# Two batches' first projections as one Strassen-Winograd product, in a fused attention and MLP kernel

## The chip, the cores and the metric

The kernel runs on one core of a Trainium2 chip. The metric is device time in microseconds (us); the kernel before takes 426.1 us (median of three runs, 425.94 to 427.35). The profiled execution, on which every reading below rests, spans 425.5 us at a mean TensorE clock of 0.992 of full speed. The engines are called as the profile calls them: PE is TensorE (PEld its weight loads), DVE is VectorE, ACT is ScalarE, POOL is GpSimd, SP is the engine that issues most transfers.

## What is computed

An attention with normalised queries and keys over 8 batches, 12 heads, 448 tokens and 64 elements a head, then an MLP on the 3584 tokens of width 768, with 2048 hidden columns and a gated activation.

```python
# q, k, v: (8, 12, 448, 64); w_in: (768, 2048); w_out: (2048, 768)
q_n, k_n = rmsnorm(q, g_q), rmsnorm(k, g_k)
attn = softmax(q_n @ k_n.T / 8) @ v                    # per batch and head
x = attn.transpose(0, 2, 1, 3).reshape(3584, 768)
h = x @ w_in                                           # the first projection
g = h * (1.0 / (1.0 + np.exp(-1.702 * h)))
out = g @ w_out                                        # the second projection
```

## The kernel before

Two heads make a pair, so there are 48 pairs, six per batch. Each pair is loaded, normalised, transposed and taken through scores, exponentials and values; six finished pairs make one batch's `xT` (768 x 448, as six blocks of 128 rows). Matrix products take bfloat16 operands and accumulate in float32.

Nothing is emitted in source order. Every piece of work is a task with an engine, an assumed duration, dependencies and a priority, and a small list scheduler written in the kernel's Python decides the order in which the instructions enter the program. The priorities (a table of 2,194 numbers named `KEYS`), the earliest starts of loads (`AT`) and a set of tasks that use another engine than the default one (`ON`) were found by a search. The hardware then runs each engine's instructions in that fixed order, each waiting for its own inputs.

```python
# the first projection of batch b, 128 hidden columns m, and what follows
def first(b, m, kis):
    if kis[0] == 0:
        gps[b, m] = bank()                          # one PSUM bank
    for j, (f, lo, n) in enumerate(blocks(b, m)):   # for b > 0: one block, n = 448
        for ki in kis:                              # 6 of them
            nc.tensor.matmul(gps[b, m][:, j * SH:j * SH + n],
                             lhsT=w_in_s[:, ki, f * 128:(f + 1) * 128],
                             rhs=xT[b][:, ki, lo:lo + n], start=(ki == 0), stop=(ki == KI - 1))

def tanh(b, m):
    th = ths[b, m] = th_p.tile([128, S], FP32, tag="th", name="th")
    nc.scalar.activation(out=th[:, :], in_=gps[b, m][:, :S], func=ACT.Tanh, scale=0.851)

def gate(b, m):                                     # g = (tanh + 1) * h; the 0.5 comes at the end
    ...
    nc.vector.scalar_tensor_tensor(
        out=g_of[b // 2][:, f:f + len(g), lo:lo + n], in0=view(ths.pop((b, m))[:, :]),
        scalar=1.0, in1=view(gps.pop((b, m))[:, :S]), op0=ALU.add, op1=ALU.mult)

# pairs from 12 on are transposed by a transfer; their q is multiplied by g on ScalarE
def scale_q(i):
    t = qk_ring[turn(i, N_KZ, K_KZ)][:, 0]
    nc.scalar.activation(out=t, in_=t, func=ACT.Identity, scale=gG[:, :])

# matmuls without use, put into gaps of TensorE early in the kernel, so that its clock stays up
FILL, FILL_GAPS = 0.9, 0.6
def fill(idle, now):
    ...
    n = idle * FILL / 213 if now < 14000.0 else idle * FILL_GAPS / 110
    for _ in range(int(n)):
        nc.tensor.matmul(banks[2][:, :256], lhsT=ident[:, :], rhs=zeros[:, :], start=True, stop=True)
```

The second projection is already a Strassen-Winograd product from batch 1 on. It takes two blocks of 128 tokens at a time (`pair`), with seven products of eight 128x384 matmuls where the plain way has eight. Its sums of `g` are made on VectorE (`add_up`), the combinations of `w_out` once (`combine`). Results that several outputs share stay in one PSUM bank, are copied out, and the next product is accumulated on top. The orders in which the parts enter are short lists; `FINAL` is that of the last two batches.

```python
EVEN = order("As A1 A2 A5 A6 C0 A7 C1 A4 A3")
MIDDLE = order("As A1 A2 A5 A6 C2 A7 C3 A4 A3 Bs B1 B2 B5 B6 D0 B7 D1 B4 B3")
FINAL = order("As A1 B1 A2 A5 A6 C2 A7 Bs C3 A4 A3 B2 B6 B5 B7 B8 B4")
```

Of the kernel before, what the change touches and what calls it, by code (L numbers as in the profile page):

```python
# [26 lines left out]
class _Order:  # L27
# [198 lines left out]
    'g': -8.99, 'gT': -17.52, 'gG': 7.12, ('S', 0, 0): 48.69, ('R', 0, 0): 7.11, ('S', 0, 1):  # L226
    60.39, ('R', 0, 1): 11.55, ('Q', 0): 58.96, ('N', 0, 0): 66.3, ('N', 0, 1): 7.12, ('V', 0):
    64.11, ('T', 0, 0): -21.71, ('T', 0, 1): -16.49, ('KQ', 0): 14.75, ('K', 0): 13.48, ('S', 1,
    0): 60.38, ('R', 1, 0): -9.0, ('S', 1, 1): 51.98, ('R', 1, 1): 17.35, ('Q', 1): 58.97, ('N',
    1, 0): 69.37, ('N', 1, 1): 66.3, ('V', 1): 7.13, ('T', 1, 0): 51.1, ('T', 1, 1): -27.7,  # L230
    ('KQ', 1): -1.35, ('K', 1): 4.81, ('S', 2, 0): 58.98, ('R', 2, 0): 13.51, ('Q', 2): 58.7,
    ('N', 2, 0): 70, ('N', 2, 1): -23.02, ('V', 2): 60.28, ('T', 2, 0): 28.84, ('T', 2, 1):
    -21.72, ('KQ', 2): 3.26, ('K', 2): -10.77, ('S', 3, 0): 67.81, ('R', 3, 0): 23.51, ('Q', 3):
    58.99, ('N', 3, 0): 66.13, ('N', 3, 1): 6.04, ('V', 3): -2.35, ('T', 3, 0): 51.09, ('T', 3,
    1): 40.36, ('KQ', 3): 5.81, ('K', 3): -15.4, ('S', 4, 0): 68.26, ('R', 4, 0): 7.79, ('Q',
    4): 47.82, ('N', 4, 0): 70, ('N', 4, 1): -17.48, ('V', 4): 58.38, ('T', 4, 0): -11.68, ('T',
    4, 1): 35.03, ('KQ', 4): 3.28, ('K', 4): 3.79, ('S', 5, 0): 68.27, ('R', 5, 0): -17.48,
    ('Q', 5): 47.88, ('N', 5, 0): 32.37, ('N', 5, 1): 4.32, ('V', 5): 56.71, ('T', 5, 0):
    -13.72, ('T', 5, 1): 46.07, ('KQ', 5): 3.27, ('K', 5): 10.41, ('L', 6, 0): -36.46, ('L', 6,
    1): -30.62, ('L', 6, 2): -30.26, ('S', 6, 0): 56.02, ('R', 6, 0): -10.86, ('N', 6, 0):  # L240
    63.85, ('N', 6, 1): -24.56, ('V', 6): -8.75, ('T', 6, 0): -26.04, ('T', 6, 1): -15.74,
    ('KQ', 6): 60.01, ('K', 6): 55.83, ('L', 7, 0): -33.93, ('L', 7, 1): -36.65, ('L', 7, 2):
    -30.27, ('S', 7, 0): 61.95, ('R', 7, 0): 53.79, ('N', 7, 0): 33.51, ('N', 7, 1): 37.76,
    ('V', 7): 1.98, ('T', 7, 0): 30.53, ('T', 7, 1): 19.28, ('KQ', 7): 70, ('K', 7): 69.99,
    ('L', 8, 0): -31.47, ('L', 8, 1): -30.61, ('L', 8, 2): -21.79, ('S', 8, 0): 66.7, ('R', 8,
    0): 15.23, ('Q0', 8): 11.01, ('Q', 8): -20.67, ('N', 8, 0): 33.53, ('N', 8, 1): -24.55,
    ('V', 8): 1.99, ('T', 8, 0): 25.89, ('T', 8, 1): -26.03, ('KQ', 8): 70, ('K', 8): 62.1,
    ('L', 9, 0): -22.78, ('L', 9, 1): -1.99, ('L', 9, 2): 21.48, ('S', 9, 0): -0.06, ('R', 9,
    0): 64.25, ('N', 9, 0): -14.38, ('N', 9, 1): -14.72, ('V', 9): 38.61, ('T', 9, 0): 6.15,
    ('T', 9, 1): -7.29, ('KQ', 9): 26.68, ('K', 9): 11.06, ('L', 10, 0): -2.06, ('L', 10, 1):  # L250
    -31.62, ('L', 10, 2): -30.35, ('S', 10, 0): 65.29, ('R', 10, 0): 56.16, ('N', 10, 0): -5.2,
    ('N', 10, 1): 8.16, ('V', 10): 60.31, ('T', 10, 0): -3.07, ('T', 10, 1): 15.45, ('KQ', 10):
    21.0, ('K', 10): 26.52, ('L', 11, 0): -1.91, ('L', 11, 1): 9.45, ('L', 11, 2): 3.39, ('S',
    11, 0): 38.83, ('R', 11, 0): 9.16, ('Q0', 11): 9.17, ('Q', 11): 14.55, ('N', 11, 0): -8.55,
    ('N', 11, 1): -8.56, ('V', 11): 32.03, ('T', 11, 0): -28.56, ('T', 11, 1): -11.34, ('KQ',
    11): 26.68, ('K', 11): -4.75, ('C', 0, 0, 0): 34.74, ('E', 0, 0, 0): 70, ('C', 0, 0, 1):
    37.36, ('E', 0, 0, 1): 58.69, ('P', 0, 0, 0, 0): -16.98, ('P', 0, 0, 0, 1): -33.13, ('P', 0,
    0, 0, 2): -27.68, ('P', 0, 0, 0, 3): 37.5, ('O', 0, 0, 0): -10.77, ('B', 0, 0): -11.23,
    ('X', 0, 0): -10.78, ('C', 1, 0, 0): -11.08, ('E', 1, 0, 0): 58.69, ('C', 1, 0, 1): 60.18,
    ('E', 1, 0, 1): 68.27, ('P', 1, 0, 0, 0): -21.73, ('P', 1, 0, 0, 1): 38.67, ('P', 1, 0, 0,  # L260
    2): -11.3, ('P', 1, 0, 0, 3): -29.83, ('O', 1, 0, 0): 3.27, ('B', 1, 0): 37.69, ('X', 1, 0):
    1.43, ('C', 2, 0, 0): 30.87, ('E', 2, 0, 0): 49.27, ('C', 2, 0, 1): 39.88, ('E', 2, 0, 1):
    69.95, ('P', 2, 0, 0, 0): -11.24, ('P', 2, 0, 0, 1): -11.3, ('P', 2, 0, 0, 2): 37.46, ('P',
    2, 0, 0, 3): 31.02, ('O', 2, 0, 0): 3.28, ('B', 2, 0): 17.36, ('X', 2, 0): -17.49, ('C', 3,
    0, 0): -18.24, ('E', 3, 0, 0): 67.04, ('C', 3, 0, 1): 50.92, ('E', 3, 0, 1): 47.91, ('P', 3,
    0, 0, 0): 31.97, ('P', 3, 0, 0, 1): -12.34, ('P', 3, 0, 0, 2): -13.73, ('P', 3, 0, 0, 3):
    32.17, ('O', 3, 0, 0): 3.05, ('B', 3, 0): -11.62, ('X', 3, 0): 6.39, ('C', 4, 0, 0): 33.09,
    ('E', 4, 0, 0): 66.44, ('C', 4, 0, 1): -27.1, ('E', 4, 0, 1): 66.38, ('P', 4, 0, 0, 0):
    32.0, ('P', 4, 0, 0, 1): -9.02, ('P', 4, 0, 0, 2): 29.97, ('P', 4, 0, 0, 3): 64.71, ('O', 4,
    0, 0): -10.87, ('B', 4, 0): 50.01, ('X', 4, 0): -0.66, ('C', 5, 0, 0): -25.89, ('E', 5, 0,  # L270
    0): 66.27, ('C', 5, 0, 1): -29.85, ('E', 5, 0, 1): 48.61, ('P', 5, 0, 0, 0): -10.94, ('P',
    5, 0, 0, 1): -29.62, ('P', 5, 0, 0, 2): -22.05, ('P', 5, 0, 0, 3): -16.54, ('O', 5, 0, 0):
    -7.38, ('B', 5, 0): -31.04, ('X', 5, 0): 2.32, ('C', 0, 1, 0): -20.61, ('E', 0, 1, 0):
    39.25, ('C', 0, 1, 1): 43.58, ('E', 0, 1, 1): 66.79, ('P', 0, 1, 0, 0): -11.67, ('P', 0, 1,
    0, 1): -13.09, ('P', 0, 1, 0, 2): 50.02, ('P', 0, 1, 0, 3): -27.45, ('O', 0, 1, 0): -11.7,
    ('B', 0, 1): 13.7, ('X', 0, 1): 7.23, ('C', 1, 1, 0): -36.95, ('E', 1, 1, 0): 45.11, ('C',
    1, 1, 1): 27.45, ('E', 1, 1, 1): 49.86, ('P', 1, 1, 0, 0): 15.35, ('P', 1, 1, 0, 1): -11.14,
    ('P', 1, 1, 0, 2): 49.86, ('P', 1, 1, 0, 3): -10.43, ('O', 1, 1, 0): 3.77, ('B', 1, 1):
    -14.37, ('X', 1, 1): 61.57, ('C', 2, 1, 0): -29.61, ('E', 2, 1, 0): 31.97, ('C', 2, 1, 1):
    -13.61, ('E', 2, 1, 1): 55.11, ('P', 2, 1, 0, 0): -4.79, ('P', 2, 1, 0, 1): -26.92, ('P', 2,  # L280
    1, 0, 2): -0.62, ('P', 2, 1, 0, 3): 14.23, ('O', 2, 1, 0): 2.31, ('B', 2, 1): 12.76, ('X',
    2, 1): 61.62, ('C', 3, 1, 0): -9.15, ('E', 3, 1, 0): 49.88, ('C', 3, 1, 1): 29.49, ('E', 3,
    1, 1): -5.68, ('P', 3, 1, 0, 0): -20.47, ('P', 3, 1, 0, 1): -26.35, ('P', 3, 1, 0, 2):
    -3.45, ('P', 3, 1, 0, 3): -26.51, ('O', 3, 1, 0): 56.03, ('B', 3, 1): -0.42, ('X', 3, 1):
    64.25, ('C', 4, 1, 0): 2.8, ('E', 4, 1, 0): 67.06, ('C', 4, 1, 1): -11.13, ('E', 4, 1, 1):
    40.1, ('P', 4, 1, 0, 0): 8.28, ('P', 4, 1, 0, 1): 4.99, ('P', 4, 1, 0, 2): 3.29, ('P', 4, 1,
    0, 3): -10.4, ('O', 4, 1, 0): 57.66, ('B', 4, 1): 25.6, ('X', 4, 1): 52.71, ('C', 5, 1, 0):
    -27.46, ('E', 5, 1, 0): 65.24, ('C', 5, 1, 1): -8.91, ('E', 5, 1, 1): 59.07, ('P', 5, 1, 0,
    0): 21.04, ('P', 5, 1, 0, 1): -24.61, ('P', 5, 1, 0, 2): 31.7, ('P', 5, 1, 0, 3): 19.29,
    ('O', 5, 1, 0): 52.63, ('B', 5, 1): -15.73, ('X', 5, 1): 56.53, ('C', 6, None, 0): 16.59,  # L290
    ('E', 6, None, 0): 52.49, ('E', 6, None, 1): -39.65, ('C', 6, None, 2): 4.04, ('E', 6, None,
    2): -4.25, ('E', 6, None, 3): -4.26, ('P', 6, None, 0, 0): -3.9, ('P', 6, None, 0, 1):
    -37.8, ('P', 6, None, 0, 2): -0.46, ('P', 6, None, 0, 3): -25.6, ('O', 6, None, 0): 52.95,
    ('P', 6, None, 1, 0): 1.59, ('P', 6, None, 1, 1): -0.0, ('P', 6, None, 1, 2): 7.1, ('P', 6,
    None, 1, 3): 14.16, ('O', 6, None, 1): 44.94, ('B', 6, None): -29.08, ('X', 6, None): 44.9,
    ('C', 7, None, 0): -15.8, ('E', 7, None, 0): -37.98, ('E', 7, None, 1): -37.64, ('C', 7,
    None, 2): -28.54, ('E', 7, None, 2): -36.42, ('E', 7, None, 3): -19.56, ('P', 7, None, 0,
    0): -2.06, ('P', 7, None, 0, 1): -27.45, ('P', 7, None, 0, 2): -27.46, ('P', 7, None, 0, 3):
# [543 lines left out]
def kernel(  # L842
# [635 lines left out]
    def copy_out(frm, bp, tm, hf):  # L1478
        nc.scalar.mul(half_of(bp, tm, hf), held[frm], 0.5)
# [249 lines left out]
```

## Time and profile before

| | busy us | share of the span |
|---|---|---|
| PE | 409.6 | 96% |
| PEld | 239.9 | 56% |
| DVE | 313.4 | 74% |
| ACT | 295.4 | 69% |
| POOL | 179.7 | 42% |

A row of the profile names the source line, the engine, what is written from what, the shape, the count, then busy time and the mean duration of one, then the engine's idle time before these instructions and what ended it. Busy time of PE counts pipelined matmuls to their modelled ends, so two matmuls that follow each other overlap in it. In a timeline the distance from one start to the next shows the pace; the printed length includes the depth of the pipeline. The rows and stages that the argument needs are shown with it below.

### The profile page before, as it was taken

To read this page: it belongs to the slowest core of one execution; us is meant where nothing else is said; L and a number is where in the kernel's file an instruction comes from. 1 tells how busy PE (TensorE), PEld (TensorE's weight loads), DVE (VectorE), ACT (ScalarE), POOL (GpSimd) and SP (SyncE) were. 2 spreads that over 40 slices of the span, in tenths; PEclk is the share of its full clock that TensorE was granted. 3 is DMA by queue.
4 is the path that set the end of the run, shared out by engine and by line. 5 is a ranking of instruction groups with operands and counts; after the bars stand their busy time and mean duration, and the time that the engine had idled before them with its cause. 6 is when DMAs were issued, how large, how long until landed. Compare 5 with 4: busy or idle time off the path is not lost.

```text
span 425.5 us, 9982 instructions
## 1 busy us (share of the span) xinstructions
PE 409.6 (96%) x3859; PEld 239.9 (56%) x3859; DVE 313.4 (74%) x608; ACT 295.4 (69%) x432; POOL 179.7 (42%) x258
## 2 busy tenths in 40 slices
PE   6989899999999999899999999999999999999995
PEld 4657787564455554565456655555555655555553
DVE  4878789569987979876898787875766655644663
ACT  4898587889979688858877788787966477304400
POOL 4677967674276887552553233242511000000000
PEclk9799999999999999999999999999999999999999
DMA  8999999869368787579657865467435450130023
GB/s 200 237 254 246 248 262 241 199 146 187 78 147 182 181 232 166 131 162 216 154 128 171 209 179 141 100 150 181 91 79 128 123 99 13 23 89 16 0 76 93
DMA packets 101556, 63.38 MB, mean 149 GB/s; under 512 B 54916, under 2 KB 101508, under 8 KB 101508
## 3 DMA queue, kind: packets, MB, share of 16 engines
q1 hardware_dynamic: 93712, 55.88, 55.3%
q0 software_dynamic: 7296, 6.29, 9.1%
q8 instruction: 30, 0.49, 0.5%
q10 hardware_dynamic: 500, 0.57, 0.4%
q14 instruction: 18, 0.15, 0.1%
HBM read 45.61 MB, written 11.01 MB: 133 GB/s over the span
## 4 chain that ended last, share of the span: by engine, by line
PE 76%; DVE 10%; DMA 9%; issue 2%; ACT 1%; POOL 1%; SPq 0%; DVEq 0%; ACTq 0%
PE w L1379 24%; PE w L1469 22%; PE o L1168 10%; PE sc L1147 8%; DMA w_in_s<-in_moe_w_in_dram 4%; PE sc L1379 4%; PE w L1409 3%; DVE g L1401 3%; PE sc L1469 2%; DMA late<-in_v_dram 2%; DVE late L1449 2%; DMA raw<-in_k_dram 1%; ACT th L1389 1%; DMA raw<-in_q_dram 1%; DVE ssq L1038 1%
## 5 line engine op out<-in xcount | busy, mean ns | idle before, releaser
L1155 ACT ACTIVATE att<-sc 112x896 bf16<-112x896 f32 x168 | 145.4, 915 | 33.0 <-PE sc L1147 32.4
L1379 PE MATMUL w<-xt,w_in_s 128*128 128x448 bf16 (+1 forms) x780 | 141.8, 329 | 2.5 <-DMA w_in_s<-in_moe_w_in_dram 1.4
L1379 PEld LDWEIGHTS <-w_in_s 128*128 128x128 bf16 x864 | 79.9, 98 | 62.1 <-issue 8.5
L1401 DVE SCALAR_TENSOR_TENSOR g<-th,w 128x448 bf16<-128x448 f32 x114 | 68.8, 616 | 26.5 <-ACT th L1389 26.1
L1080 POOL TENSOR_TENSOR row<-raw,rs 112x512 bf16<-112x512 f32 x65 | 72.3, 1130 | 31.2 <-DMA qk<-row 19.5
L1168 PEld LDWEIGHTS <-att 112*128 112x128 bf16 x1536 | 63.2, 98 | 31.3 <-issue 10.6
L1389 ACT ACTIVATE th<-w 128x448 f32<-128x448 f32 x114 | 61.4, 545 | 25.0 <-PE w L1379 22.6
L1038 DVE TENSOR_REDUCE ssq<-sq 112x16 f32<-112x1024 f32 (+1 forms) x50 | 58.2, 1170 | 11.5 <-ACT sq L1029 10.0
L1168 PE MATMUL o<-vx,att 112*128 112x65 bf16 x1280 | 60.7, 195 | 1.9 <-DVE obs L1179 1.9
L1093 POOL TENSOR_TENSOR vx<-vraw,ones 112x512 bf16<-112x512 f32 x22 | 23.8, 1082 | 89.7 <-PE o L1168 70.4
L1147 PE MATMUL sc<-qk 64*128 64x448 bf16 (+1 forms) x360 | 47.6, 344 | 0.1
L1469 PEld LDWEIGHTS <-g 128*128 128x128 bf16 x336 | 30.9, 98 | 22.2 <-issue 3.3
L1179 DVE TENSOR_TENSOR obs<-o,rcp 112x256 bf16<-112x256 f32 x96 | 40.8, 424 | 3.3
L1469 PEld LDWEIGHTS <-late 128*128 128x128 bf16 x328 | 29.9, 98 | 22.6 <-issue 4.0
L1029 ACT ACTIVATE sq<-raw 112x1024 f32<-112x1024 f32 (+1 forms) x32 | 31.8, 1002 | 5.8 <-DMA raw<-in_q_dram 4.3
L1469 PE MATMUL w<-w_out_s,g 128*128 128x384 bf16 x192 | 35.8, 326 | 0.0
L1178 DVE RECIPROCAL rcp<-o 112x4 f32<-112x4 f32 x96 | 17.0, 177 | 22.4 <-PE o L1168 22.0
L1026 POOL TENSOR_TENSOR sq<-raw 112x1024 f32<-112x1024 f32 x14 | 26.9, 1922 | 10.7 <-DMA raw<-in_k_dram 7.5
L1469 PE MATMUL w<-late 128*128 128x384 bf16 x152 | 28.5, 326 | 0.0
L1469 PE MATMUL w<-w_out_s,late 128*128 128x384 bf16 x144 | 27.5, 326 | 0.0
L1070 POOL TENSOR_TENSOR t<-rs 112x48 f32<-112x48 f32 x28 | 8.2, 292 | 42.5 <-DVE rs L1059 28.6
L1389 ACT ACTIVATE th<-sc 128x448 f32<-128x448 f32 x14 | 7.6, 543 | 26.5 <-PE sc L1379 21.7
(89 smaller groups left out, 436.8 us busy)
## 6 DMA issues: line engine op xcount, KB each, us to landing
raw<-in_q_dram SPq DMA_DIRECT2D x44, 224.0 KB, 3.8
raw<-in_k_dram SPq DMA_DIRECT2D x43, 224.0 KB, 4.3
vraw<-in_v_dram SPq DMA_DIRECT2D x42, 224.0 KB, 3.8
w_in_s<-in_moe_w_in_dram POOLq DMA_DIRECT2D x4, 768.0 KB, 15.0
w_out_s<-in_moe_w_out_dram POOLq DMA_DIRECT2D x4, 768.0 KB, 19.6
out_dram<-osb SPq DMA_DIRECT2D x13, 168.0 KB, 3.2
out_dram<-osb SPq DMA_DIRECT2D x12, 144.0 KB, 3.7
out_dram<-osb SPq DMA_DIRECT2D x12, 120.0 KB, 2.0
```

The lines of the kernel that those rows point to most:

```text
L1026: nc.gpsimd.tensor_tensor(out=sq[i % N_SQ][:SS, part], in0=raw[turn(i, N_RAW, K_RAW)][:SS, part], in1=raw[turn(i, N_RAW, K_RAW)][:SS, part ...
L1029: nc.scalar.activation(out=sq[i % N_SQ][:SS, part], in_=raw[turn(i, N_RAW, K_RAW)][:SS, part], func=ACT.Square)
L1038: nc.vector.reduce_sum(out=ssq_of[g0][:SS, i - g0, part], in_=sq[i % N_SQ][:SS, part], axis=AX.X)
L1080: eng.tensor_tensor(out=row_ring[i % N_QKN][:SS, gi].rearrange("p n (h d) -> p h n d", h=2), in0=raw[turn(i, N_RAW, K_RAW)][:SS, gi], in1= ...
L1147: nc.tensor.matmul(sc[:, hp, j * SH:j * SH + n], lhsT=qkw[r, k0:k0 + WIN], rhs=qk[r, 0, qs], start=True, stop=True)
L1155: nc.scalar.activation(out=att[:SS, t, :, :S], in_=sc, func=ACT.Exp)
L1168: nc.tensor.matmul(os_[u, w][:, x, :], lhsT=att_of(u)[:SS, kc, hp, qs * SS:qs * SS + WIN], rhs=vx_ring[turn(i, N_V, K_V)][:SS, hp, kc, :], ...
L1179: nc.vector.tensor_tensor(out=to[:SS, :, w, :] if h is None else to[:SS, :2].rearrange("p n h d -> p (n h) d"), in0=o[:SS, :, :D], in1=rcp ...
L1379: nc.tensor.matmul(gps[b, m][:, j * SH:j * SH + n], lhsT=w_in_s[:, ki, f * 128:(f + 1) * 128], rhs=xT[b][:, ki, lo:lo + n], start=(ki == 0 ...
L1389: nc.scalar.activation(out=th[:, :], in_=gps[b, m][:, :S], func=ACT.Tanh, scale=0.851)
L1401: nc.vector.scalar_tensor_tensor(out=g_of[b // 2][:, f:f + len(g), lo:lo + n], in0=view(ths.pop((b, m))[:, :]), scalar=1.0, in1=view(gps.p ...
L1469: nc.tensor.matmul(held[to], lhsT=lhs[:, ko, :], rhs=y[:, ko, :], start=first and ko == 0, stop=ko == NK - 1, skip_group_check=not first)
```

## The change

The first projections of batches 6 and 7 (called `B0` and `B1` in the code) become one product. Its two-by-two blocks are the two batches, the two halves of the 768 input columns and the two halves of the 2048 hidden columns. Strassen-Winograd forms it with seven block products in place of eight. A block product is, for 128 hidden columns `n` of eight, three matmuls of 128x448. Combinations of `w_in` (`w_term`) and of the two `xT` (`x_term`) are made on VectorE, in the space of the raw inputs once the attention no longer needs them.

```diff
+    W11, W21, W12, W22 = [w_in_s[:, KH * c:KH * c + KH, FH * r:FH * r + FH] ...]
+    W_TERMS = ((W3, W11, W21, ALU.subtract), (W21, W21, W22, ALU.add), (W2, W21, W11, ALU.subtract),
+               (W4, W12, W2, ALU.subtract))
+    def w_term(j, h):                  # j of 4, half h of 2: each 128 x 1536 bfloat16
+        ...
+        nc.vector.tensor_tensor(out=o, in0=x, in1=y, op=op)
+    def x_term(j):                     # 4 of them, each 128 x 1344 bfloat16
+        o, x, y = ((X1, x_half(B1, 0), x_half(B0, 0)),
+                   (x_half(B1, 0), x_half(B1, 1), x_half(B1, 0)),
+                   (X2, x_half(B1, 1), X1), (X4, x_half(B0, 1), X2))[j]
+        nc.vector.tensor_tensor(out=o, in0=x, in1=y, op=ALU.subtract)
+    def joint_product(n, j, to, first):
+        if first:
+            joint[n, to] = bank()
+        w, x = ((W11, x_half(B0, 0)), (W12, x_half(B0, 1)), (W4, x_half(B1, 1)), (W22, X4),
+                (W21, X1), (W2, X2), (W3, x_half(B1, 0)))[j - 1]
+        for ki in range(KH):           # KH = 3
+            nc.tensor.matmul(joint[n, to][:, :S], lhsT=w[:, ki, n * 128:(n + 1) * 128],
+                             rhs=x[:, ki, :], start=first and ki == 0, stop=ki == KH - 1, ...)
```

Products 1, 6, 7 and 4 share one bank. After 1, 6 and 7 the running sum is copied out (`part_copy`, by ScalarE or VectorE, as the scheduler picks); VectorE then adds another bank to the copy (`part_add`), and ScalarE makes the gelu in one instruction (`gelu`) from that sum, or from the bank itself after product 4. The two-step tanh and gate of these batches are gone, a second set of activation tables is loaded once, after the last exponential, and the last two batches' outputs no longer need the factor 0.5.

```diff
+    def gelu(b, f, src):
+        nc.scalar.activation(out=g_of[B // 2 - 1][:, f, (b - B0) * S:(b - B0 + 1) * S], in_=src(),
+                             func=ACT.Gelu_apprx_sigmoid)
-    FINAL = order("As A1 B1 A2 A5 A6 C2 A7 Bs C3 A4 A3 B2 B6 B5 B7 B8 B4")
+    for n in range(NF := MI // 2):     # 8 columns, staggered
+        FINAL += [(n, 1), (n, 2)] * (n > 0) + [(n - 2, 3)] * (n > 1) + [(n - 1, 7)] * (n > 0)
+        FINAL += [(n, 5), (n, 6)] + [(n - 1, 4)] * (n > 0)
+    FINAL += [(NF - 2, 3)] + order("Ax") + [(NF - 1, 7)] + order("Bx") + [(NF - 1, 4), (NF - 1, 3)]
+    FINAL += order("Ex Au Bu Ay Av By Bv As A5 A6 Ey A7 E2 A4 A3 Bs B5 B6 C0 B7 C1 B4 B3 Es C2 E6 C3 "
+                   "E5 E7 E8 E4")
```

The product of q with g moves to VectorE, and the fill ahead of 14 us grows.

```diff
-        nc.scalar.activation(out=t, in_=t, func=ACT.Identity, scale=gG[:, :])
+        nc.vector.tensor_scalar(out=t, in0=t, scalar1=gG[:, :], scalar2=None, op0=ALU.mult)
-    FILL, FILL_GAPS = 0.9, 0.6
+    FILL, FILL_GAPS = 1.2, 0.6
-    osb_ring = ring("osb", 6, [128, HALF], FP32)
+    osb_ring = ring("osb", 5, [128, S], FP32)
...
-    PACE = 5800.0
+    PACE, PACE_2, TURN = 5800.0, 4700.0, 71000.0
+    def now_key():
+        return 10.3 + min(done, TURN) / PACE + max(done - TURN, 0.0) / PACE_2
```

With these tasks the search over priorities, earliest starts and engines was run anew: all 2,194 old priorities have new values, and 49 are added. The `ON` set moves single normalisations, squares and casts between VectorE, GpSimd and ScalarE. Normalisations on VectorE go from 25 to 31, casts of v there from 20 to 18, squares on GpSimd from 15 to 12 (the rest run on ScalarE). Of the weight loads, which go through one queue one after the other, the earliest starts in the scheduler's table are these, in us:

| | w_in 0 | 1 | 2 | 3 | w_out 0 | 1 | 2 | 3 |
|---|---|---|---|---|---|---|---|---|
| before | 11.2 | 15.4 | 24.8 | 0 | 10.4 | 53.0 | 18.3 | 0 |
| after | 11.0 | 6.3 | 25.1 | 25.4 | 29.6 | 53.0 | 44.1 | 46.0 |

A later load in the chain can't start ahead of an earlier one, whatever its own entry.

## The prediction

> **What bounds the kernel now.** I read the page's busy shares first, then the TensorE timeline of the last stage, then who TensorE waited for, and last the windows early and late, to see what room the other engines have.
>
> On the page, TensorE is near full and everything else is not:
>
> ```profile
> PE 409.6 (96%) x3859; PEld 239.9 (56%) x3859; DVE 313.4 (74%) x608; ACT 295.4 (69%) x432; POOL 179.7 (42%) x258
> PE   6989899999999999899999999999999999999995
> PEclk9799999999999999999999999999999999999999
> ```
>
> A busy PE counts pipelined ends, so I checked it in the timeline of PE between 380 and 402 us (start, length, line, matmuls):
>
> ```profile
> 380.87 2.43 PE L1379 MATMUL sc<-xt,w_in_s 128*128 128x448 bf16 x12
> 383.13 2.43 PE L1379 MATMUL w<-xt,w_in_s 128*128 128x448 bf16 x12
> 385.40 1.30 PE L1379 MATMUL sc<-xt,w_in_s 128*128 128x448 bf16 x6
> 386.54 1.30 PE L1379 MATMUL w<-xt,w_in_s 128*128 128x448 bf16 x6
> 387.99 3.57 PE L1379 MATMUL sc<-xt,w_in_s 128*128 128x448 bf16 x18 [0.15 <-DVE g L1401]
> ...
> 399.65 2.76 PE L1469 MATMUL w<-w_out_s,g 128*128 128x384 bf16 x16
> 402.25 1.46 PE L1469 MATMUL sc<-w_out_s,g 128*128 128x384 bf16 x8
> ```
>
> Six matmuls of 448 columns take 386.54 - 385.40 = 1.14 us from start to start, 0.189 each; sixteen of 384 take 402.25 - 399.65 = 2.60, 0.1625 each. The groups touch. This stage runs at TensorE's pace, so a matmul less is its time less. From start distances over the whole timeline (start, plus length, less the 0.165 us by which touching groups overlap) I sum 14 us in which TensorE did nothing: 8.4 before 60 us, 3.8 between 100 and 180, 1.8 after 360. Its longest waits by name:
>
> ```profile
> PE o L1168 <- DVE obs L1179: 1.9, 4, 1.2
> PE w L1194 <- DVE obs L1179: 1.4, 2, 1.0
> ...
> PE w L1379 <- DMA w_in_s<-in_moe_w_in_dram: 1.4, 1, 1.4
> ...
> PE w L1379 <- DVE g L1401: 1.1, 3, 0.5
> ```
>
> Early on there is waste that isn't idle: the 74 fill matmuls on the page, 15.0 us busy and all before 35 us, while the first useful projection starts at 35.98 us. By their start distances they fill about 10 us. The last matmul ends near 421.2 us, and the last copy and store take the remaining 4.3.
>
> **What the Trainium skill says.** "TensorE: Matmul & The Clock Gate", section Part 1 on the clock gate, gives the warm start-to-start time as columns over 2.4 GHz plus about 2.5 ns. That is 189 and 162.5 ns for the two widths here; the trace agrees with both. "ScalarE: Activation LUTs", section "What ACT_TABLE_LOAD costs", says that every function costs the same per element, 186 ns plus 0.833 ns an element with immediate scale: 559 ns for 448, as an estimate for the new gelu. The trace has 545 for the tanh that it replaces, and two table loads of 1283 ns each. "VectorE: DVE Perf Modes" says in "Side-by-side" that a one-source bfloat16 operation in SBUF can take four elements a cycle with about 150 cycles of overhead: (112 + 158)/0.96 = 281 ns as an estimate for q times g. No run yet shows that form; the trace has ScalarE at 668 ns for it.
>
> **The change part by part.**
>
> *Matmuls.* Removed: 2 batches x 16 x 6 = 192 of 448 columns. Added: 8 x 7 x 3 = 168. The second projections keep their number, 3 pairs x 7 x 8 + 4 x 8 = 200 for the last two batches. So 24 x 0.189 = 4.54 us less on TensorE, all on the path.
>
> *New sums of inputs, on VectorE.* 8 `w_term` of 1536: the present combinations of w_out have this shape at 1147 ns (two of them 1692), so 8 x 1.15 = 9.2 us. 4 `x_term`, three of 1344: a 1024 sum takes 687 ns when not disturbed, hence 0.85 each, 3.4 in all. Only the last `x_term`s depend on the end of the attention.
>
> *Gates to gelus.* 32 gates x 0.616 = 19.7 us leave VectorE; 24 adds of the same shape come, 24 x 0.62 = 14.9. ScalarE changes 32 tanh for 32 gelus at the same cost, takes part of 24 copies (0.55 each) and one table load of 1.28.
>
> *q times g.* 36 x 0.668 = 24.0 us leave ScalarE; 36 x 0.28 = 10.1 come to VectorE.
>
> *Engines chosen anew.* Six more normalisations on VectorE (918 ns: +5.5), two casts less (680 ns: -1.4); three more squares on ScalarE (+3.0).
>
> *Where these land.* From the joint product on, TensorE has 168 x 0.189 + 200 x 0.1625 = 31.8 + 32.5 = 64.3 us of work without any attention in it. If the last matmul ends at 421.2 - 4.5 = 416.7, the joint product must start by about 352 us, whereas the attention's last values now run at 372.5. Two windows up to that point:
>
> ```profile
> 0.00:372.00 372.00, 361.34 (x3570) 212.91 (x3571) 285.75 (x559) 285.58 (x413) 179.65 (x258) 0.99 0.72 163
> 372.00:425.50 53.50, 48.30 (x291) 27.01 (x288) 27.66 (x50) 9.84 (x19) 0.00 (x0) 1.00 0.20 54
> ```
>
> VectorE (third pair) and ScalarE (fourth) both stand at 286 of 372, 77%. After: VectorE in all 313.4 + 9.2 + 3.4 - 19.7 + 14.9 + 10.1 + 5.5 - 1.4 = 335; less what follows the start of the joint product (24 adds 14.9, 13 sums x 0.69 = 9.0, some 18 output copies and adds x 0.557 = 10.0), 301 of 352, 86%. ScalarE: 295.4 - 24.0 + 3.0 + 6 (half the copies) = 280, less 32 x 0.55, the copies and a few outputs, 27: 253 of 352, 72%. So ScalarE gains room and VectorE loses it; it stays below its stage's length, but with less slack for TensorE's needs. In the joint stage itself one column block takes TensorE 21 x 0.189 = 3.97 us, against ScalarE's 4 x 0.55 + 1.5 x 0.55 = 3.0 and VectorE's 3 x 0.62 + 1.5 x 0.55 = 2.7. Both fit.
>
> *The chain in one bank.* A copy must end before the next product goes on top: about 0.1 + 0.55 + 0.1 us. The order leaves four other products (2.27 us) after products 1 and 6, but only two (1.14 us) between 7 and 4. That holds if the copy starts at once. A gelu ahead of it on ScalarE can cost some 0.3 us, at worst in each of eight blocks: 0 to 2.4 us; I take 0.8. At the end, product 3 of the last block needs add and gelu (0.62 + 0.56 + waits, 1.6 us); the second projections that don't need it last 1.95 us. Covered.
>
> *Start of the joint product.* `x_term` after the last transposed block, 3 us of transfer and 3 x 0.85 us on VectorE, is covered only if the order keeps enough second projections of batch 5 for it. The list places four products of 1.3 us there, with the new first two products among them. I put down 0.7 us lost.
>
> *New order.* It may win part of the 14 us idle and 10 us fill: the third and fourth w_in loads are allowed 3 us earlier than they were issued (28.4 and 29.3 us), and the 1.4 us wait for them should go. The stage between 100 and 180 us, where VectorE is at 84 to 97%, gets 0.28 us per pair more on VectorE and can lose. Net guess: 2.2 us won.
>
> The sum: 426.1 - 4.5 + 0.8 + 0.7 - 2.2 + 0.5 (more early fill and VectorE slack) = 420.6.
>
> **Rivals.**
>
> *VectorE becomes the bound in the middle.* For it: 86% on the mean, 19.37 busy of 20 us already between 100 and 120, and TensorE's idle time there is put down to VectorE's divide and gate. Against it: TensorE has other batches' work to run meanwhile, and the order was searched with these loads in it. It would eat 4 to 7 us: 424 to 428.
>
> *The attention can't be finished 20 us earlier, or the joint product stalls on its chain.* For it: everything after 352 us is one dependent stretch. Against it: TensorE loses just 1.8 us in today's last 65 us, which has chains of the same kind. It would cost 3 to 6 us: 423 to 427.
>
> *The new order wins much in the start.* For it: 35 us before the first projection, with 18 us idle or in fill. Against it: the first 75 us move 200 to 260 GB/s in every slice and the transfer engines are full, and the weight loads aren't moved much. It would give 416 to 418.
>
> *Nothing but the matmuls counts.* Then 421.5.
>
> **Range and chances.** All but the rivals' extremes fall between 416.8 and 425.2, which I take as the range. A gain over 2% means below 417.6, which needs 4 us beyond the matmuls: chance 0.13. Over 2% slower means above 434.6: neither rival gets there; 0.02. The rest, 0.85, is within 2%.
>
> **What would show it.** Joint matmuls at 0.189 us, 168 of them, with TensorE's groups touching after 352 us (less than 4 us idle in all): the saving is real. ScalarE's q row gone, a VectorE row near 280 ns x36. Gelus near 560 ns and a third table load. The attention's last values near 350 us. The first useful projection at or before 36 us. It would be wrong if TensorE's waits name the copies or sums of the joint product for more than 3 us, if its idle time between 60 and 350 us rises above 6 us behind VectorE, or if the first projection starts some 4 us earlier or later than now.

## The result and the profile after

| | median us | executions |
|---|---|---|
| before | 426.02 | 425.53 to 427.35 |
| after | 430.83 | 430.55 to 432.31 |

The ratio is 1.0115, with a 95% interval of [1.0083, 1.0147]. The change costs 4.8 us where the prediction expected a gain of 5.5, and the time lies outside the predicted range. It is still within 2% of the kernel before, which the prediction held likeliest, but on the other side.

TensorE has less work and takes longer over it. These are its busy line, its slices and its granted clock on the page of the kernel after:

```profile
PE 407.6 (95%) x3852; PEld 236.6 (55%) x3852; DVE 342.9 (80%) x673; ACT 282.1 (66%) x403; POOL 171.0 (40%) x251
PE   7889899998999999999999999999999999889895
PEclk9999999999999999999999999999999999999999
```

The mean clock is 1.000. Where the kernel before has nines up to the last slice, there is a dip near the end (8, 8, 9, 8 in slices 35 to 38, some 365 to 408 us).

Where does TensorE stop? I take the distance from the start of one matmul to the start of the next, less the usual distance of that shape (0.189 us for 448 columns, 0.1625 for 384). Where more than 0.1 us is left, I call it a stop. The stops add up like this by stage:

| TensorE's stops, us | 0 to 60 | 60 to 120 | 120 to 340 | 340 to end | last matmul starts |
|---|---|---|---|---|---|
| before | 8.3 | 2.2 | 2.0 | 1.8 | 420.85 |
| after | 9.9 | 4.1 | 1.4 | 8.7 | 424.35 |

The first column can't be compared as it stands, because fill matmuls take up time that would otherwise be a stop, and their own usual distance differs (0.213 us in the execution before, 0.119 after). All time up to 60 us above the usual distances of the useful matmuls, fill included, is 26.4 us before and 26.1 after, so that stage is unchanged. The rest adds up: -0.3 + 1.9 - 0.6 + 6.9 in stops, -4.5 of matmuls saved, +3.4 in all; the last matmul starts 3.5 us later. (The profiled execution of the kernel before, at 427.26 us and a mean clock of 0.992, is itself 1.2 us above that kernel's median, which brings the 3.5 close to the 4.8.)

So the loss sits in the last 90 us, in the stage that was to bring the gain. The timeline of PE of the kernel after in the joint product (start, length, line, tiles, shape, count, and in brackets the idle time ahead of the group with what ended it):

```profile
365.20 0.73 PE L1717 MATMUL w<-rows,w_in_s 128*128 128x448 bf16 x3
365.77 0.73 PE L1717 MATMUL sc<-rows 128*128 128x448 bf16 x3
367.32 0.73 PE L1717 MATMUL sc<-rows,w_in_s 128*128 128x448 bf16 x3 [0.82 <-DVE osb L1731]
```

Touching groups of three lie 0.57 us apart, the predicted 3 x 0.189. But 365.77 to 367.32 is 1.55 us: 0.98 lost. (The bracket says 0.82 because modelled ends overlap the next start by 0.165 us.) The same timeline in the second projections at the end, where the two kernels do the same work:

```profile
411.10 1.46 PE L1483 MATMUL sc<-late,g 128*128 128x384 bf16 x8
412.39 0.81 PE L1483 MATMUL sc<-w_out_s,sq 128*128 128x384 bf16 x4
413.85 0.81 PE L1483 MATMUL sc<-w_out_s,sq 128*128 128x384 bf16 x4 [0.65 <-DVE osb L1496]
```

Here a product of eight matmuls is broken in the middle. Matmuls 1 to 4 go into a bank, matmul 5 of the same product into the same bank starts 0.81 us late. Nothing in the product's own inputs or bank asks for that. It waits for VectorE at L1496, which empties another bank. The VectorE instruction, in the timeline of DVE, waited in turn for TensorE:

```profile
413.24 0.56 DVE L1496 TENSOR_SCALAR osb<-sc 128x384 f32<-128x384 f32 x1 [1.49 <-PE sc L1483]
```

The waits of PE by name (total us, times, longest) put the stops down to VectorE's and ScalarE's readers of PSUM, and nearly all of the waiting matmuls write `sc`:

```profile
PE sc L1717 <- DVE att L1731: 1.1, 2, 0.8
PE sc L1717 <- DVE osb L1731: 1.1, 2, 0.8
PE sc L1483 <- DVE att L1501: 0.9, 2, 0.6
...
PE sc L1483 <- DVE att L1496: 0.6, 1, 0.6
PE sc L1483 <- DVE osb L1496: 0.6, 1, 0.6
...
PE sc L1483 <- ACT osb L1493: 0.6, 1, 0.6
```

**What `sc` is.** The name was in the "before" timeline of the prediction as well; I had not asked what it stands for. It is the score tile of the attention, and it spans two banks:

```python
    banks = [ps_w.tile([128, 512], FP32, ...) for j in range(3)]        # w: one bank each
    sc_ring = [ps_sc.tile([128, 2, 512], FP32, ...) for j in range(2)]  # sc: two banks each
    banks += [t[:, j, :] for t in sc_ring for j in range(2)]            # halves, lent out late
```

When the scores are done, the four halves serve as four more banks for products. A product has its half to itself, but the program's order of accesses is kept by tile. This is, in short form, the piece of the compiled program around the stop at 413.85 us, with the waits in it (the numbers are places in the program):

```
9809  TensorE  matmul 4 of 8 into sc1, second half
9810  VectorE  copy of sc1, first half (L1496)       waits for 9809
9812  TensorE  matmul 5 of 8 into sc1, second half   waits for 9810
```

VectorE's copy of the first half waits for the matmul just ahead of it into the *second* half; the matmul after it waits for the copy. TensorE then pays a full hand-over there and back, 0.56 us of copy with 0.04 us ahead of it and 0.05 behind it (413.20 to 413.85), although the two never touch the same bank. In the compiled kernel after, 24 matmuls wait for a reader of the other half (17 times VectorE, 7 times ScalarE). In the kernel before it is 10.

Not each of them costs time. Put one by one beside the timeline, 12 of the 24 are stops, with 6.4 us together; the other 12 find their reader done. Another 0.79 us, at 398.49 us, is the same wait at one remove: that matmul needs a bank whose copy was itself ordered behind matmuls into the other half. That leaves 1.5 of the 8.7 us to other causes.

The other engines, in two windows (length, then busy us and count of PE, PEld, DVE, ACT and POOL, the clock, DMA share, GB/s):

```profile
0.00:352.00 352.00, 340.49 (x3482) 200.64 (x3483) 293.59 (x590) 262.04 (x365) 170.98 (x251) 1.00 0.75 170
352.00:429.00 77.00, 67.07 (x371) 35.99 (x369) 49.34 (x84) 20.06 (x38) 0.00 (x0) 1.00 0.16 44
```

The stage up to 352 us is close to the prediction, with VectorE at 294 of 352. The last stage has 64.3 us of matmuls in 77 us.

### The profile page after: what moved, and what is told of

Same layout as the page of the kernel before. It is cut to its first block, busy times and chain, and to the rows that moved or that the text cites. A ratio compares the mean times of both kernels' runs of the same rounds, so it can differ in the third digit from the quotient of the medians.

```text
span 429.0 us, 9991 instructions
## 1 busy us (share of the span) xinstructions
PE 407.6 (95%) x3852; PEld 236.6 (55%) x3852; DVE 342.9 (80%) x673; ACT 282.1 (66%) x403; POOL 171.0 (40%) x251
## 4 chain that ended last, share of the span: by engine, by line
PE 71%; DVE 17%; ACT 3%; DMA 3%; POOL 2%; issue 2%; SPq 0%; DVEq 0%; POOLq 0%; ACTq 0%
PE w L1392 21%; PE w L1483 20%; PE o L1181 9%; PE sc L1160 9%; PE sc L1483 6%; PE sc L1717 2%; PE w L1717 2%; DVE row L1093 2%; PE w L1422 2%; DVE late L1463 2%; ACT att L1170 1%; DVE ssq L1051 1%; DMA rows<-in_v_dram 1%; DVE obs L1192 1%; DVE g L1414 1%
## 5 line engine op out<-in xcount | busy, mean ns | idle before, releaser
L1392 PE MATMUL w<-xt,w_in_s 128*128 128x448 bf16 (+1 forms) x672 | 119.8, 326 | 0.7 <-DVE g L1414 0.7
L1392 PEld LDWEIGHTS <-w_in_s 128*128 128x128 bf16 x672 | 61.2, 98 | 42.3 <-issue 7.0
L1093 POOL TENSOR_TENSOR row<-rows,rs 112x512 bf16<-112x512 f32 x62 | 69.8, 1146 | 30.8 <-DMA qk<-row 25.1
L1402 ACT ACTIVATE th<-w 128x448 f32<-128x448 f32 x96 | 52.7, 552 | 27.1 <-PE w L1392 25.1
L1414 DVE SCALAR_TENSOR_TENSOR g<-th,w 128x448 bf16<-128x448 f32 x96 | 57.5, 614 | 15.6 <-ACT th L1402 15.4
L1106 POOL TENSOR_TENSOR vx<-rows,ones 112x512 bf16<-112x512 f32 x21 | 22.0, 1046 | 55.3 <-PE o L1181 33.0
L1042 ACT ACTIVATE sq<-rows 112x1024 f32<-112x1024 f32 (+1 forms) x35 | 35.4, 1017 | 7.1 <-DMA rows<-in_q_dram 4.5
L1039 POOL TENSOR_TENSOR sq<-rows 112x1024 f32<-112x1024 f32 x11 | 21.2, 1931 | 13.9 <-DMA rows<-in_k_dram 4.9
L1093 DVE TENSOR_TENSOR row<-rows,rs 112x512 bf16<-112x512 f32 x26 | 25.3, 981 | 0.9 <-POOL rs L1086 0.9
L1737 ACT ACTIVATE g<-att 128x448 bf16<-128x448 f32 x19 | 10.8, 577 | 17.3 <-DVE att L1731 17.3
```

The costliest lines, as they stand in the source:

```text
L1042: nc.scalar.activation(out=sq[i % N_SQ][:SS, part], in_=raw[turn(i, N_RAW, K_RAW)][:SS, part], func=ACT.Square)
L1093: eng.tensor_tensor(out=row_ring[i % N_QKN][:SS, gi].rearrange("p n (h d) -> p h n d", h=2), in0=raw[turn(i, N_RAW, K_RAW)][:SS, gi], in1= ...
L1106: nc.gpsimd.tensor_tensor(out=vx[:, :, :D], in0=vr, in1=ones[:SS, :].to_broadcast([SS, 2 * NS, D]), op=ALU.mult)
L1392: nc.tensor.matmul(gps[b, m][:, j * SH:j * SH + n], lhsT=w_in_s[:, ki, f * 128:(f + 1) * 128], rhs=xT[b][:, ki, lo:lo + n], start=(ki == 0 ...
L1414: nc.vector.scalar_tensor_tensor(out=g_of[b // 2][:, f:f + len(g), lo:lo + n], in0=view(ths.pop((b, m))[:, :]), scalar=1.0, in1=view(gps.p ...
```

## The experiments

My theory (A) is that the loss after 340 us comes from the waits across the two halves of a tile, and goes when every product has a one-bank tile. The first rival is the chain inside the shared bank, where the copies sit mostly on VectorE (22 of 24) behind adds and sums; then the loss goes when ScalarE copies. The second rival is the start of the joint product with its sums of inputs. Besides these stand the smaller suspects of the middle and the start: q times g on VectorE, the searched order, and the fill.

### One-bank tiles, and copies on ScalarE

`after_single` and `before_single` keep each kernel's order on every engine. Once all exponentials are done, the pool of the score tiles is given back and four one-bank tiles, called `n`, are taken in its place:

```diff
-    ps_sc = pool("ps_sc", 1, space=PSUM)
+    ps_two = tc.tile_pool(name="ps_sc", bufs=1, space=PSUM); ps_sc = ps_two.__enter__()
...
-            od.add("late", "none", 0, lambda: None, 0, widen=[("w", len(banks))],
-                   deps=[("E", NG - 1, None, t) for t in range(NS)])
+            od.add("late", "none", 0, one_bank, 0, widen=[("w", len(banks))],
+                   deps=[("E", i, None, t) for i in range(NP, NG) for t in range(NS)])
```

(`one_bank` leaves `ps_two`, opens a pool of four [128, 512] tiles and puts them into `banks[3:7]`.) `after_act` leaves the banks alone and gives every copy of the joint product to ScalarE; `after_single_act` has both edits:

```diff
-        if by_v:
+        if by_v and False:
             nc.vector.tensor_copy(out=part_of[n, j], in_=joint[n, "a"][:, :S])
```

> The changed kernel, with the same order of instructions on every engine; only the four late PSUM banks become four tiles of one bank each once the attention is over, where before they are halves of two tiles of two banks. Theory A (the lost time is waits between the two halves of a tile, which the program orders although they are different banks): the stops of TensorE after 340 us fall from about 9 us to under 3, the four mid-product stops of 0.8 us in the last 32 us are gone, and the time falls by 5 to 7 us, to about 424 to 426 us. Theory B (VectorE is overloaded in the joint stage, 24 adds and 22 of 24 copies on it): the stops stay, the time falls by less than 1.5 us. Theory C (the loss is in the re-searched order of the first 340 us): no change.

> The kernel before with one-bank tiles after the attention, order unchanged. Theory A: it has only a few such waits (0.3, 0.3, 0.3 and 0.6 us after 360 us), so it gains 1 to 1.7 us, to about 424.7. Theories B and C: no change (within 0.5 us).

> The changed kernel with all 24 copies of the joint stage on ScalarE at the places in the order where they stand now; banks as they are. Theory B: VectorE loses 22 x 0.62 = 13.6 us in a stage of 35 us, the stops in the joint stage (about 5 us from 350 to 390) mostly go, 3 to 5 us gained. Theory A: the waits between halves stay, only on another engine; less than 1.5 us gained or lost. Theory C: no change.

> Both: one-bank tiles and all copies on ScalarE. Theory A: within 1 us of the one-bank tiles alone. Theory B: most of the gain is here and with the copies alone. If both count, this is the fastest by more than 1 us, near 423.

| beside a before of 425.64 us | median us | ratio | stops 340 to end |
|---|---|---|---|
| `after_single` | 423.81 | 0.9962 [0.9945, 0.9979] | 1.7 |
| `before_single` | 423.70 | 0.9953 [0.9934, 0.9971] | 0.0 |
| `after_act` | 429.85 | 1.0115 [1.0068, 1.0163] | 8.7 |
| `after_single_act` | 423.20 | 0.9945 [0.9926, 0.9964] | 1.6 |

One-bank tiles take 7.0 us off the kernel after (430.83 to 423.81; 6.5 by the ratios, because the two were timed in different comparisons), with no instruction moved, and 1.9 off the kernel before. Moving the copies alone leaves the stops at 8.7 us and the ratio where it was, so the rival of the chain falls. The same stretch of the timeline of PE in `after_single`:

```profile
365.35 0.73 PE L1717 MATMUL w<-rows,w_in_s 128*128 128x448 bf16 x3
365.91 0.73 PE L1717 MATMUL n<-rows 128*128 128x448 bf16 x3
366.48 0.73 PE L1717 MATMUL n<-rows,w_in_s 128*128 128x448 bf16 x3
```

The groups that were 1.55 us apart are now 0.57 apart. And in `before_single` the small gap ahead of 387.99 us, which the prediction's timeline of the kernel before shows with 0.15 us, is gone too:

```profile
384.17 1.30 PE L1379 MATMUL w<-xt,w_in_s 128*128 128x448 bf16 x6
385.31 3.57 PE L1379 MATMUL n<-xt,w_in_s 128*128 128x448 bf16 x18
```

Of the 1.8 us that the kernel before loses late, 1.5 were this wait already: four of its ten are stops. The rest is one stop of 0.33 us at 372.54, where the attention's values wait for VectorE.

### The same wait, made more and less frequent

If the waits are the cause, choosing the bank by what its tile's other half is doing must move the time both ways, with everything else in place. `after_mates` prefers a bank whose other half is free; `before_shared` seeks one whose other half is in use. Both keep their kernel's order. The key compares whether the other half is busy first, then which is free longest; `before_shared` turns the first part of the key round:

```diff
                         self.got = min(self._open(best.takes[0], now),
-                                       key=lambda j: held[j] and self.named[held[j]].end or 0.0)
+                                       key=lambda j: self._rank(best.takes[0], held, j, now))
```

> The changed kernel, order unchanged, tiles of two banks kept, but a bank is taken whose other half is free wherever there is one. The matmuls that wait for the reader of the other half go from 24 to 10. Theory A: most of the 7 us of the one-bank tiles come back, 424.5 to 427. If the gain of the one-bank tiles came from something else in giving back and taking PSUM anew: no change, near 430.8.

> The kernel before, order and number of instructions unchanged, but whenever a bank is chosen, one is taken whose other half of the tile is in use. The matmuls that wait for the reader of the other half go from 10 to 33. Theory A (waits between the halves): 3 to 7 us slower than before, with stops of TensorE after 360 us and names of DVE or ACT in them. If the number of a bank doesn't matter: no change.

| | matmuls that wait for the other half | stops 340 to end, us | median us |
|---|---|---|---|
| `before_single` | 0 | 0.0 | 423.70 |
| before | 10 | 1.8 | 425.99 |
| `before_shared` | 33 | 12.2 | 436.62 |
| `after_single` | 0 | 1.7 | 423.81 |
| `after_mates` | 10 | 3.6 | 426.03 |
| after | 24 | 8.7 | 430.83 |

The ratios to before are 1.0259 [1.0224, 1.0295] for `before_shared` and 1.0002 [0.9989, 1.0016] for `after_mates`. The kernel before has no joint product at all, and is slowed by 10.6 us, more than the 3 to 7 expected, with nothing but another choice among free banks. Its timeline of PE then shows broken products like those of the kernel after:

```profile
423.21 0.81 PE L1469 MATMUL sc<-w_out_s,late 128*128 128x384 bf16 x4
424.67 0.81 PE L1469 MATMUL sc<-w_out_s,late 128*128 128x384 bf16 x4 [0.65 <-DVE att L1482]
...
426.78 0.81 PE L1469 MATMUL sc<-late,sq 128*128 128x384 bf16 x4 [0.65 <-DVE att L1487]
```

Each such stop is 0.65 us in the bracket, 0.81 by the start distances. Not every wait costs that much: the 7.0 us of stops that one-bank tiles remove (8.7 less 1.7) are 0.29 on the mean of 24. Those waits are the cause of the loss in the last stage. (`after_mates` has as many waits as before, but only 1.0 of its 3.6 us of stops is theirs.)

### What the matmuls are worth

`sa_twice` starts from `after_single_act` and computes product 2 of every column block twice, 24 more matmuls of 448 columns; the bank is started afresh for the second time, so that the product counts once:

```diff
-        for ki in range(KH):
+        for ki in list(range(KH)) * (2 if j == 2 else 1):
```

> The same version with product 2 of every column block computed twice (24 matmuls of 448 columns more, the second computation replaces the first, the output is unchanged). This puts back on TensorE just the work that Strassen saves. If the stage runs at TensorE's pace: 24 x 0.189 = 4.5 us slower, about 427.7. If the saving is taken up by waits anyway: under 2 us slower.

The median is 427.92 (ratio to before 1.0053 [1.003, 1.0076]) against 423.2: 4.7 us for 24 matmuls, where 24 x 0.189 is 4.54. The two were not timed beside each other, and the profiled executions differ by 3.7 us, with 0.6 us less of stops after 340 us in `sa_twice`. So most or all of a joint matmul's time is on the path, and the saving is real.

### q times g back on ScalarE

`after_qg` undoes this part in the kernel after, `sa_qg` in `after_single_act`; the instructions keep their places:

```diff
-        nc.vector.tensor_scalar(out=t, in0=t, scalar1=gG[:, :], scalar2=None, op0=ALU.mult)
+        nc.scalar.activation(out=t, in_=t, func=ACT.Identity, scale=gG[:, :])
```

> The changed kernel with nothing but q times g put back on ScalarE. Theory D: 1 to 2 us faster, about 429.3, the stops between 60 and 120 us fall by some 2 us, those after 340 us stay as they are.

> The version with one-bank tiles and copies on ScalarE (423.2 us), with q times g put back on ScalarE at the same places in the order. It takes 36 x 0.38 = 13.7 us from VectorE and gives ScalarE 36 x 0.67 = 24 us. Theory D (q times g on VectorE causes the stops of TensorE between 60 and 120 us, which are 2 us more than in the kernel before with one-bank tiles): these stops fall by 1 us or more and the time by 1 to 2 us. Rival (the order was found for VectorE, and ScalarE's exponentials then come later): the stops move to waits for exponentials, the time is the same or up to 2 us worse.

`after_qg` takes 428.81 us (1.007 [1.0044, 1.0096]), 2.0 less than after; its stops between 60 and 120 us fall from 4.1 to 2.3, before's level, and those after 340 us stay at 8.7. `sa_qg` takes 421.90 us (0.9904 [0.9874, 0.9935]), 1.3 less than its base, with 2.3 instead of 4.1 in that stage. (Neither was timed beside its base.) The windows of the kernel after around there (length; PE, PEld, DVE, ACT, POOL):

```profile
80.00:100.00 20.00, 18.99 (x221) 10.78 (x220) 19.34 (x36) 16.50 (x23) 9.79 (x13) 1.00 0.72 185
100.00:120.00 20.00, 18.14 (x177) 9.21 (x175) 19.69 (x37) 16.40 (x24) 8.14 (x14) 1.00 0.31 63
```

and of `after_qg`:

```profile
80.00:100.00 20.00, 19.96 (x239) 11.76 (x238) 18.98 (x35) 19.01 (x26) 12.23 (x15) 1.00 0.66 174
100.00:120.00 20.00, 18.59 (x183) 9.70 (x182) 19.34 (x36) 18.13 (x28) 8.73 (x14) 1.00 0.38 84
```

In the kernel after VectorE is 97 and 98% full there while ScalarE has 18% free. With the product back on ScalarE the work is more even, and TensorE does 24 more instructions in the 40 us. So in this short stage VectorE holds TensorE up.

### The combinations of the weights

Is the start of the joint product bound by VectorE's sums, as the second rival has it? `sa_wt` gives half of the `w_term` instructions to GpSimd, which stands idle after 340 us:

```diff
-        nc.vector.tensor_tensor(out=o, in0=x, in1=y, op=op)
+        (nc.gpsimd if h else nc.vector).tensor_tensor(out=o, in0=x, in1=y, op=op)
```

> The same version with the second half of the four combinations of w_in (needed only from the fifth column block on) on GpSimd, which is idle by then. VectorE has 3.8 us less between 340 and 355 us. Theory E (the joint product starts late because VectorE still makes combinations while the last values wait for it): the 1.5 us of stops between 345 and 356 us fall under 0.7 and the time by about 1 us. Rival: GpSimd takes so long for a combination (some 3 us each) that the second half of the joint product waits, or slows VectorE; same time or up to 2 us worse.

The median is 428.93 (1.0067 [1.0041, 1.0093]), 5.7 us more than its base and well above the 2 us of the run's own rival. From the timelines of POOL and DVE in `sa_wt`:

```profile
340.38 3.42 POOL L1701 TENSOR_TENSOR rows<-w_in_s 128x1536 bf16<-128x1536 bf16 x1
343.88 3.58 POOL L1701 TENSOR_TENSOR rows<-w_in_s,rows 128x1536 bf16<-128x1536 bf16 x1
```

```profile
345.45 2.83 DVE L1701 TENSOR_TENSOR rows<-w_in_s 128x1536 bf16<-128x1536 bf16 x1
```

GpSimd takes 3.4 us for what VectorE does in 0.95, and a combination left on VectorE, which ran beside one of GpSimd, took 2.83. It was one of four bfloat16 sums of VectorE beside GpSimd's four; the others took 3.73, 1.98 and 2.14 us for the usual 0.68, 0.68 and 0.85. Each of the four ended 0.54 to 0.82 us after the GpSimd instruction beside it had ended. So VectorE lost some 7.5 us there where 3.8 were taken off it. TensorE stops four times between 336 and 350 us, 1.17 to 1.90 us each, ahead of groups of the attention's values. The run thus made VectorE slower in this stretch, and shows that slower sums are dear there. It does not test whether faster sums would gain: with one-bank tiles only about 1.6 us of stops are left after 340 us.

### The order and the fill

`sa_old` runs `after_single_act` with the table of priorities, the starts and the choices of engine of the kernel before. The two tables of priorities have 2,125 tasks in common; 69 of the kernel before are gone in the kernel after, and 118 are new there (the 49 named with the change are the difference). In `sa_old` these 118, among them all of the joint product, have no entry and take the priority that the code gives by default.

```diff
-KEYS, AT, ON = <searched anew with the joint product>
+KEYS, AT, ON = <those of the kernel before; the new tasks have none>
```

> The same version with the kernel before's priorities, earliest starts and choice of engines for all tasks that both have, so that the search is undone and the structure stays. Theory F (the new order costs the early stage and the stage from 60 to 120 us some 3 us): those stages come back to what the kernel before has, but the attention then ends some 15 us later than the joint product needs it, so that TensorE stands still ahead of the joint product; 425 to 435 us in all, with stops of 5 us or more around 350 to 380 us. Rival (the search brings nothing): about 423.

It takes 477.47 us (1.1211 [1.1159, 1.1263]), far above the 425 to 435 expected. The longest waits of PE in it:

```profile
PE o L1172 <- DVE obs L1183: 13.7, 18, 1.9
PE sc L1151 <- ACT att L1159: 12.2, 12, 1.9
```

As I read it, the old order leaves attention to be done beside the last batches' projections, which is what it was searched for; the joint product cannot start until the attention is over, and so the attention then runs alone and waits for its own readers. Part of the loss is clock, with a mean of 0.942 in the profiled execution and 0.79 between 340 and 420 us. The new structure needs an order of its own, but this run mixes that need with the loss of the search, and with new tasks whose priorities were never searched for. It doesn't say what the new order is worth.

`sa_qg_fill` is `sa_qg` with the old fill:

```diff
-    FILL, FILL_GAPS = 1.2, 0.6
+    FILL, FILL_GAPS = 0.9, 0.6
```

> The version with one-bank tiles, copies and q times g on ScalarE (421.9 us), with the fill ahead of 14 us as before (0.9 for 1.2). If the larger fill saves the early clock: up to 1 us slower, with a granted clock under 1 before 15 us. If it is of no weight: the same within 0.5 us.

The median is 421.46 (0.9906 [0.9873, 0.9939]) against 421.90 in another comparison: no difference to be seen. The fill is meant to keep TensorE's clock up. In the profiled execution of `sa_qg_fill` the granted clock is 0.90 up to 10 us, 0.51 between 10 and 15, and 1.00 from 15 to 20 us.

From one execution to the next the mean clock differs by up to a hundredth, and in the longer series the time goes with it: over the 20 executions of `after_single` the correlation of time and mean clock is -0.84, at 3.2 us per hundredth; over the 35 of the kernel before beside it, -0.62 at 1.9. Over the 11 of the kernel before beside `sa_qg`, whose clocks lie closer together (0.991 to 0.996), no such link is to be seen (+0.16). In `sa_qg_fill` the mean over its executions is 0.9955, in `sa_qg` 0.9965, too little to tell.

## Why the prediction was wrong

**The failed step: "The chain in one bank ... I take 0.8".** This is the term of the sum for TensorE's waits within the joint product; with the 0.7 for its start, 1.5 us. Measured, the stops after 340 us grow by 6.9 us, from 1.8 to 8.7. The step looked for the wait where the program reuses a bank, and worked out copy and product within it. That part was sound: in `after_single` and in `after_single_act`, with the copies nearly all on VectorE or all on ScalarE, TensorE has no stop between 355.2 and 385.0 us, so the chain itself costs nothing that shows. What the step left out were banks that are *not* shared. With four banks in two tiles, each reader of one half is ordered among the matmuls into the other. The order picks the bank that is free longest and doesn't look at the other half. How many of these waits arise is therefore a matter of the choice of banks: `after_mates` has 10 with the same products in the same sequence, and `before_shared` has 33 without a joint product. That groups of three matmuls make such an encounter likelier than groups of six is plausible and wasn't tested.

**The signs of being wrong missed it.** The prediction wanted TensorE's groups to touch after 352 us, with less than 4 us idle; the stops there are 8.1 us, and this sign did show. Of the three that it named for being wrong, none came. The waits that name copies or sums of the joint product come to 2.2 us (L1731), not to more than 3, since the rest name the readers of the second projection.

**The rival's counter-evidence misled me.** I held against a stall after 352 us that "TensorE loses just 1.8 us in today's last 65 us, which has chains of the same kind". Those 1.8 us were not the price of chains; `before_single` has the same chains and loses 0.0. Of them, 1.5 were waits of exactly the harmful kind, four of ten, and with the change the ten became 24. The rival foresaw a stall in this stage; its 3 to 6 us were too small, and its cause was another.

**"24 x 0.189 = 4.54 us ... all on the path": right.** The joint groups run at 0.57 us for three, and `sa_twice` measures 4.7 by the medians.

**"Net guess: 2.2 us won" by the new order: wrong.** The start is unchanged (26.4 against 26.1 us above the useful matmuls; first useful projection at 35.04 after, 35.98 before). Between 60 and 120 us the stops grow by 1.9, and `after_qg` shows q times g as the cause. The prediction saw this risk ("the stage between 100 and 180 us ... can lose") and gave it 0.5 us in the sum.

**"Start of the joint product: 0.7 lost": under-sized.** Of the 1.7 us of stops that `after_single` keeps after 340 us, 1.3 lie here, between 348 and 356 us. Half of that is one stop that ends at 353.07, where a second projection waits for a sum of outputs on VectorE (L1501) that stands in line behind the combinations of w_in.

**Sizes.** Predicted 560 ns for a gelu; measured 526 to 533 from PSUM and 577 from SBUF. The third table load is there with 1283. `w_term` was put at 1150 ns and takes 954. q times g was put at 281 and has a median of 328. Half of the copies were to be ScalarE's; 22 of 24 are VectorE's at 0.62 us, which puts 49.3 us instead of some 34 on it after 352 us, without harm. Two of these rows, from the groups of the kernel after (busy us and mean ns, then the idle time ahead and its releaser):

```profile
L1134 DVE TENSOR_SCALAR qk<-qk,gG 128x448 bf16<-128x448 bf16 x36 | 13.6, 382 | 0.0
L1737 ACT ACTIVATE g<-att 128x448 bf16<-128x448 f32 x19 | 10.8, 577 | 17.3 <-DVE att L1731 17.3
```

**The attention by about 350 us: right.** Its last values run at 345.98, with VectorE busy 294 us (301 predicted) and ScalarE 262 (253 predicted) of the first 352.

**The sum, put right.** The prediction's own terms come to 421.4, not to the 420.6 that it states; its gain was 4.7 us by them. With the measured sizes: 426.1 - 4.5 + 6.9 (stops after 340 us, 8.7 less 1.8) + 1.9 (60 to 120 us) - 0.6 (120 to 340 us) - 0.3 (start) = 429.5, against 430.83 measured; the missing 1.3 is about the distance of before's profiled execution from its median.

**What is left of the gain.** With the waits gone and q times g back, the joint product beats the old way by 1.8 us (`sa_qg` 421.90 against `before_single` 423.70, not timed beside each other, and single executions overlap), not by 4.5. In the two profiled executions (421.25 and 423.70 us) TensorE's last matmul starts 2.45 us earlier, and most of that can be placed: 4.5 us less of matmuls, 1.6 us more of stops after 340 us, and 0.4 us more before that. The 1.8 is smaller because the profiled execution of `sa_qg` is 0.65 us below its median.

**What stays open.** What the order is worth by itself, and whether a search with one-bank tiles would close the gap, wasn't tried.

The version to keep is `sa_qg`: one-bank tiles, copies and q times g on ScalarE, 421.90 us, 0.9904 [0.9874, 0.9935] of before's time, and some 9 us under after, beside which it wasn't timed.

## What to carry to other kernels

In these kernels a PSUM tile that spans two banks is one thing to the order of accesses, even when its halves serve unrelated products, and that cost up to 7 us. Give every product a tile of one bank, and hand the large tile back when its own use is over. When a product is broken in the middle in TensorE's timeline, look at which tile the releaser reads, not only at which engine it is. And before a small loss is taken as the price of today's structure, ask of each of its waits what it protects: a wait that protects nothing is small only as long as it is rare.

## What the runs showed of the hardware that was not expected

- In the four longest series (20 to 35 executions) a kernel's time goes with its mean granted clock, by 1.6 to 3.2 us for each hundredth (correlation -0.56 to -0.84); over 11 executions of the kernel before it doesn't (+0.16). In the profiled execution of `sa_qg_fill` the clock missing from the mean lies within the first 15 us (0.90 up to 10 us, then 0.51).
- A sum of 128 x 1536 bfloat16 takes 3.1 to 3.6 us on GpSimd and 0.95 on VectorE. The four bfloat16 sums of VectorE that ran beside those of GpSimd took 1.98 to 3.73 us for the usual 0.68 to 0.95, and each ended 0.54 to 0.82 us after the one on GpSimd.
- The one-source bfloat16 product on VectorE that the prediction put at 281 ns has a median of 328, with single ones up to 1114 and a mean of 382; a gelu of the same width is 0.05 us quicker from PSUM (526 to 533 ns) than from SBUF (577).
